# A fused attention and bilinear feed-forward kernel: spreading weight rounding, moving the denominators and an accumulating transfer, and computing T3 earlier

## The chip, the cores and the metric

The kernel runs on one core of a Trainium2 chip. The metric is device time in microseconds (us). The engines are named as in the profile: PE is TensorE (PEld its weight loads), DVE VectorE, ACT ScalarE, POOL GpSimd, SP SyncE, which here issues most DMA transfers. Every engine works through its own instructions in the order of the program; semaphores hold an instruction until its inputs and its buffer are free.

## The reference

Routing attention, then a bilinear feed-forward layer. Cut to what is computed:

```python
# q, k, v: (4, 8, 768, 64); centroids: (8, 16, 64)
q_assign = argmax(q_n . c_n); k_assign = argmax(k_n . c_n)   # nearest of 16 centroids
mask = q_assign[..., None] == k_assign[..., None, :]
scores = where(mask, q @ k.T / 8, -1e9)
attn = softmax(scores); x = (attn @ v) as (3072, 512)
a = x @ w_a; b = x @ w_b            # (512, 1536) each
out = (a * b) @ w_out               # (1536, 512)
```

## The kernel before

Attention goes by 16 pairs of heads (four to a batch of 768 rows), each in two halves of 384 queries with six score tiles (`j` = 0 to 5). A group, one round of the main loop (`g`), handles two score tiles, so a pair takes six groups and a batch 24. The score tile comes out of PSUM through an exponential into one of four buffers `pt`; one group later the tiles are multiplied with `v`, and summed into `acc` for the softmax's denominators. From the second batch of attention on, the feed-forward products of the batch before are strewn between the attention work (`ffn` is their queue). They are done by a Strassen-Winograd scheme with seven products in place of eight; its combined operands are called S1 to S4 (weights) and T1 to T4 (rows of x).

Sums of the exponentials. For the later pairs (`p >= HP`, the second batch on), the first two tiles are added on DVE and the other four by accumulating transfers that POOL issues:

```python
def add_up(u):
    p, hf, j = where(u)
    if j == 0 or j == NJ - 1 and p < HP:
        return
    ...
    if j == 1:
        nc.vector.tensor_tensor(out=acc, in0=probs[u - 1], in1=probs[u], op=ALU.add)
    else:
        nc.gpsimd.dma_start(out=acc, in_=probs[u], accum_op=ALU.add)     # L598
```

The denominators are the sums across partitions, by products with ones (L629), copied back by ACT (L634). The tile comes from `apart()`, which, once products are due, is one of the two score tiles:

```python
def denominators(p, hf):
    ps = apart()
    acc = accs.pop((p, hf))
    ...
            nc.tensor.matmul(out=ps[a * D:(a + 1) * D, 0:HB], lhsT=ones, rhs=t[:, a, :], ...)
    nc.scalar.activation(out=den, in_=ps[:, 0:HB], func=AF.Copy, accum_out=...)
```

Rounding of the weights: 36 parts of 128x512, which arrive as 64-bit values in one of two buffers `raw`. Four DVE operations and a POOL addition make the 32-bit value; `rest` has one buffer. ACT then inspects the sizes with two activations (`see_w`), which lets the load of the part after the next start:

```python
def round_w(i):
    ...
    nc.vector.tensor_scalar(out=wi, in0=hi, ...)                  # L280
    nc.vector.scalar_tensor_tensor(out=wi, in0=hi, in1=wi, ...)   # L283
    rest = wtp.tile([P, WN], FP32, name="rest")
    nc.vector.tensor_scalar(out=rest, in0=wi, ...)                # L287
    nc.vector.scalar_tensor_tensor(out=rest, in0=lo, in1=rest, ...)   # L290
    nc.gpsimd.tensor_tensor(out=w, in0=w, in1=rest, op=ALU.add)   # L292
    unseen.append(...)

def see_w():
    while unseen:
        ...
        nc.scalar.activation(out=size, in_=upper, func=AF.Abs)    # L304
        nc.scalar.activation(out=size, in_=size, func=AF.Relu, ...)   # L306
        load_w(i + 2)
```

Two of the seven products, with the takes (ACT copies a bank out, L830), the additions (DVE, L834) and the multiplications (POOL, L840). A bank is written again by the product two places later, once the copy has read it:

```python
def take(name, k, f):
    box[name] = place(k, f)
    nc.scalar.copy(out=box[name], in_=box["X"][:, 0:HB])
    see_w()
def add(name, bank):
    nc.vector.tensor_tensor(out=box[name], in0=box[name], in1=box[bank][:, 0:HB], op=ALU.add)
def done(name, k, f):
    if not is_a:
        nc.gpsimd.tensor_tensor(out=to, in0=to, in1=box[name], op=ALU.mult)
...
def p6():
    product("X", "S2", "T2", start=False)
    take("12", 1, i)
def p7():
    product("X", "S3", "T3", start=False)
    take("22", 1, i + N2); add("22", "Z"); done("22", 1, i + N2)
...
# order [p1, p2, p6, p5, p7, p3, p4]; in the first batch:
ps[1] = both(ps[1], lambda: combine_x(b, "T3"))    # T3 behind p2
ps[3] = both(lambda: combine_x(b, "T4"), ps[3])
```

The main loop, cut:

```python
due = {3 * i + 1: [i] for i in range(8)}
for i in range(8, len(w_parts)):
    due.setdefault(26 + int((i - 8) / 1.5), []).append(i)
...
for g in range(NG + 3):
    ...
    score(now)                       # products and exponentials
    check_inverses()
    for u in before: add_up(u)
    weigh(before)
    if g % 3 == late and 0 < g - late:
        denominators(*divmod(g // 3 - 1, 2))
    ready[l]()
    parts = due.get(g, [])
    def round_next():
        if parts or not ffn:
            see_w()
        if parts:
            round_w(parts.pop(0))
    round_next()
    if halved: todo.extend(normalize(*ph))      # DVE, DVE, DVE, then POOL multiplies xT (L661)
    if ffn:
        credit += ...
        while len(ffn) > least and credit > 0:
            cost, piece = ffn.popleft(); credit -= cost
            piece()
            if todo: todo.popleft()()
            round_next()
    else:
        credit = 0
    round_next()
    while todo: todo.popleft()()
    ...
```

Of the kernel before, what the change touches and what calls it, by code (L numbers as in the profile page):

```python
# [34 lines left out]
P = 128  # L35
# [107 lines left out]
def short_path(nc, tc, ctx, c, cn, centroids_in, casts, n_far, q, k, v,  # L143
# [121 lines left out]
    def load_w(i):  # L265
        if i >= len(w_parts):
            return
        raw = rawp.tile([P, WN], INT64, name="raw")
        nc.sync.dma_start(out=raw, in_=w_parts[i][1])
        raws[i] = raw  # L270

    def round_w(i):
        w = w_parts[i][0]
        wi = w.bitcast(INT32)
        raw = raws.pop(i)
        halves = lambda dt: raw.bitcast(dt).rearrange("p (n two) -> p n two", two=2)
        lo, hi = halves(UINT32)[:, :, 0], halves(INT32)[:, :, 1]


        nc.vector.tensor_scalar(out=wi, in0=hi, scalar1=3, scalar2=0x3FFFFFF8,  # L280
                                op0=ALU.logical_shift_left,
                                op1=ALU.bitwise_and)
        nc.vector.scalar_tensor_tensor(out=wi, in0=hi, scalar=SIGN_TOP, in1=wi,  # L283
                                       op0=ALU.bitwise_and, op1=ALU.bitwise_or)

        rest = wtp.tile([P, WN], FP32, name="rest")
        nc.vector.tensor_scalar(out=rest.bitcast(INT32), in0=wi,  # L287
                                scalar1=SIGN_EXP, scalar2=None,
                                op0=ALU.bitwise_and)
        nc.vector.scalar_tensor_tensor(out=rest, in0=lo, scalar=2.0 ** -52,  # L290
                                       in1=rest, op0=ALU.mult, op1=ALU.mult)
        nc.gpsimd.tensor_tensor(out=w, in0=w, in1=rest, op=ALU.add)  # L292
        unseen.append((i, halves(FP32)[:, :, 1]))

    unseen = []

    def see_w():

        while unseen:
            i, upper = unseen.pop()
            size = spare()[0].bitcast(BF16)[:, 3 * WN:4 * WN]
            nc.scalar.activation(out=size, in_=upper, func=AF.Abs)  # L304
            n = 4 * NPAIR + i
            nc.scalar.activation(out=size, in_=size, func=AF.Relu, scale=-STEEP,  # L306
                                 bias=edge[:, 0:1], accum_out=stat[:, n:n + 1])
            load_w(i + 2)

    NSTAT = 4 * NPAIR + len(w_parts)  # L310
    edge = zero.tile([P, 1], FP32, name="edge")
# [231 lines left out]

    probs, accs, O_of, den_of, xTs = {}, {}, {}, {}, {}
    unchecked = []
    todo = deque()
    UPP = 2 * NJ
    NU = NPAIR * UPP
# [34 lines left out]
# [5 lines that stand above are left out]
            accs[p, hf] = accp.tile([P, 2, HB], FP32, name="acc")  # L588
        acc = accs[p, hf]
        if p < HP:  # L590
            nc.vector.tensor_tensor(out=acc, in0=probs[u - 1] if j == 1 else acc,  # L591
                                    in1=probs[u], op=ALU.add)
            return
        if j == 1:
            nc.vector.tensor_tensor(out=acc, in0=probs[u - 1], in1=probs[u],  # L595
                                    op=ALU.add)
        else:
            nc.gpsimd.dma_start(out=acc, in_=probs[u], accum_op=ALU.add)  # L598

    def weigh(us):  # L600
        for u in us:
# [141 lines left out]
    def spare():  # L743
        if "spare" not in W:
            W["spare"] = [combp.tile([P, n], FP32, name=name) for name, n in (
                ("pair", 2 * WN), ("comb", 2 * P))]
        return W["spare"]
# [25 lines left out]
    def combine_x(b, name):  # L773
        x = xTs[b]
        l, r = {"T3": (x[:, 2:4, HB:S], x[:, 0:2, HB:S]),
                "T1": (x[:, 0:2, HB:S], x[:, 0:2, 0:HB]),
                "T2": (x[:, 2:4, HB:S], W["T1"]),
                "T4": (x[:, 2:4, 0:HB], W["T2"])}[name]
        nc.vector.tensor_tensor(out=W[name], in0=l, in1=r, op=ALU.subtract)

    def ffn_ups(b, h):
# [109 lines left out]
        for n, (combinations, ps) in enumerate(parts):  # L891
            if n == 0 and b:
                ps[0] = both(*combinations, ps[0])
                ps[2] = both(lambda: combine_x(b, "T4"), ps[2])
            elif n == 0:
                ps[1] = both(ps[1], lambda: combine_x(b, "T3"))
                ps[3] = both(lambda: combine_x(b, "T4"), ps[3])
            if n + 1 < len(parts):
                for i, step in enumerate(parts[n + 1][0], 4):
                    ps[i] = both(ps[i], step)  # L900
            pieces += [(2 * HB, f) for f in ps]
# [10 lines left out]
    def ffn_downs(b, h):  # L912
# [96 lines left out]

        def before():  # L1010
            see_w()
            assert not raws
            down_room()
            tiles[0][0]()
            combine_w("T1", "12", "11")
            combine_w("T2", "22", "T1")
# [13 lines left out]
    def both(*fs):  # L1030
        return lambda: [f() for f in fs]
# [5 lines left out]
    def early_steps():  # L1037
        combinations = []

        def begin():  # L1040
            early_room(h_first)
            steps, pieces = ffn_ups(0, h_first)
            ups_first.extend(pieces)
            combinations.extend(steps)

        last = HP * GPP
        return {last - 8: lambda: (begin(), combine_x(0, "T1")),
                last: lambda: [f() for f in combinations[0:2]],
                last + 1: lambda: combinations[2]()}

    def ffn_ready(p, hf):

        b, hp = divmod(p, HP)
        if hp < HP - 1 or hf == 0:
            return
        if b > 0:
            h = []

            ffn.insert(len(ffn) - FREE_ROOM, (0, lambda: (
                up_room(b), combine_x(b, "T3"), combine_x(b, "T1"))))  # L1060
            ffn.insert(len(ffn) - 1, (0, lambda: combine_x(b, "T2")))
            ffn.extend(ffn_ups(b, h)[1])
        else:
            h = h_first
            combine_x(0, "T2")
            ffn.extend(ups_first + plain_ups(0, h, range(NF - 4, NF)))
        ffn.extend(ffn_downs(b, lambda: h))

# [14 lines left out]

    due = {3 * i + 1: [i] for i in range(8)}
    for i in range(8, len(w_parts)):
        due.setdefault(26 + int((i - 8) / 1.5), []).append(i)
    early = early_steps()

    for _ in range(12):
        nc.tensor.matmul(out=idle[0:D, 0:D], lhsT=ones, rhs=ones, start=True,  # L1090
# [31 lines left out]
    for g in range(NG + 3):  # L1122
        p, l = divmod(g, GPP)
        if l == 0:
            ready = prep_steps(p + 1)
        now = (2 * g, 2 * g + 1)
        before = (2 * g - 2, 2 * g - 1)
        if g == 1:
            weigh(before)
        if 0 < g < NG:  # L1130
            score(now)
        check_inverses()
        if 0 < g <= NG:
            for u in before:
                add_up(u)
        if 1 < g <= NG:
            weigh(before)
        late = int(g > EARLY)
        if g % 3 == late and 0 < g - late:
            denominators(*divmod(g // 3 - 1, 2))  # L1140
        if g < NG:
            ready[l]()
        parts = due.get(g, [])
        if g in early:
            todo.append(early[g])

        def round_next():
            if parts or not ffn:
                see_w()
            if parts:  # L1150
                i = parts.pop(0)
                round_w(i)

        round_next()
        if g <= EARLY:
            first, second = 4, 1
        else:
            first, second = 5, 3 if g < NG else 2
        ph = {first: (p, 0), second: (p - 1, 1)}.get(l)
        halved = ph in den_of  # L1160
        if halved:
            todo.extend(normalize(*ph))
        if ffn:
            credit += PER_GROUP[(g > 2 * BG + 3) + (g > 3 * BG + 3)]
            least = FREE_ROOM if halved and ph[1] and (ph[0] + 1) % HP == 0 else 0
            while len(ffn) > least and credit > 0:
                cost, piece = ffn.popleft()
                credit -= cost
                piece()
                if todo:  # L1170
                    todo.popleft()()
                round_next()
        else:
            credit = 0
        round_next()
        while todo:
            todo.popleft()()
        if halved:
            ffn_ready(*ph)
        if l == 0 and p + 1 < NPAIR:  # L1180
            if p and not by_blocks(p + 1):
                prep_transpose(p + 1, 2)
            load(p + 2)
        if l == 4 and p + 1 < NPAIR and not by_blocks(p + 1):
            prep_onehot(p + 1, 0)
# [265 lines left out]
```

## Time and profile before

| | |
|---|---|
| time, median of 3 | 1055.83 us (1055.52 to 1056.8) |
| span of the profiled execution | 1052.8 us |
| PE busy | 1023.8 us, 97% |
| DVE, ACT, POOL busy | 55%, 32%, 24% |
| accumulating transfers `acc<-pt` | 96, 384 KB each, 4.0 us to landing in the median |
| mean granted clock of TensorE | 0.995 |

PE's busy share is so high that the reading goes by its idle time: which waits it has, where in the span, and which engine's queue ended them. A line of a timeline has the start in us, the duration, the engine, the line of the kernel, the operation, what it writes and reads, and in brackets how long its engine stood idle before it and what ended that. A line of the waits has who waited for whom, the total in us, how often, and the longest.

### The profile page before, as it was taken

Reading aid. Unit: us, or ns where it says so; the run is one execution under the profiler, and the core shown is the slowest. Engines: PE = TensorE matmul, PEld = TensorE weight load, DVE = VectorE, ACT = ScalarE, POOL = GpSimd, SP = SyncE. Lnnn points to the kernel's source line nnn. Section 1 sums busy time; section 2 is a strip of 40 time slices with the busy share of each in tenths; the row PEclk is TensorE's granted clock in tenths of the full one; section 3 lists DMA queues with packets and bytes.
Section 4 is the critical chain, followed back from the end, with each engine's and each line's share of the span. In section 5 each row is a group of like instructions: output and inputs, shape, how many; then the busy total and the mean of one; then the engine's idle time right before and its main releaser. Section 6 shows DMA issues by size and latency. Waiting matters only on the chain.

```text
span 1052.8 us, 17688 instructions
## 1 busy us (share of the span) xinstructions
PE 1023.8 (97%) x7094; PEld 499.5 (47%) x7094; DVE 579.2 (55%) x1098; ACT 336.5 (32%) x674; POOL 254.1 (24%) x251
## 2 busy tenths in 40 slices
PE   8999989989999999999999999999999999999997
PEld 5443333334445554444444655444444566444564
DVE  6668777786658345443545535444443635444552
ACT  5666544444542213333233121233232201111100
POOL 1112234354332112222324211232222110212100
PEclk9999989999999999999999999999999999999999
DMA  7334546857574463626243372533322320000000
GB/s 181 87 83 88 102 90 147 167 129 154 140 156 86 94 112 65 109 46 106 54 81 65 78 134 54 91 61 66 60 45 50 76 56 21 1 1 1 6 31 29
DMA packets 134346, 84.24 MB, mean 80 GB/s; under 512 B 108144, under 2 KB 117360, under 8 KB 134256
## 3 DMA queue, kind: packets, MB, share of 16 engines
q0 software_dynamic: 13824, 37.75, 19.8%
q1 hardware_dynamic: 120016, 44.85, 19.0%
q8 instruction: 58, 0.95, 0.4%
q10 hardware_dynamic: 416, 0.43, 0.1%
q14 instruction: 32, 0.26, 0.1%
HBM read 37.78 MB, written 6.29 MB: 42 GB/s over the span
## 4 chain that ended last, share of the span: by engine, by line
PE 80%; DMA 6%; DVE 6%; issue 4%; POOL 2%; ACT 2%; DVEq 0%; POOLq 0%; SPq 0%; ACTq 0%
PE m L692 54%; PE s L563 12%; PE O L606 10%; DMA acc<-pt 5%; PE s L629 1%; PE m L629 1%; PE s L378 1%; DVE acc L591 1%; ACT pt L572 1%; PE m L378 1%; POOL xT L661 0%; DVE acc L595 0%; POOL acc L598 0%; POOL h L840 0%; PE m L362 0%
## 5 line engine op out<-in xcount | busy, mean ns | idle before, releaser
L572 ACT ACTIVATE pt<-s 128x768 f32<-128x768 f32 x192 | 146.2, 808 | 191.1 <-PE s L563 142.6
L598 POOL DMA_DIRECT2D acc<-pt x96 | 82.8, 862 | 261.1 <-DMA acc<-pt 161.5
L606 PE MATMUL O<-pt,v 128*64 128x384 f32 x768 | 145.0, 499 | 0.0
L563 PE MATMUL s<-qkT 64*128 64x384 f32 x768 | 140.3, 484 | 0.0
L840 POOL TENSOR_TENSOR h<-h,ha 128x384 f32<-128x384 f32 x66 | 72.8, 1110 | 214.6 <-DVE ha L834 213.7
L834 DVE TENSOR_TENSOR ha<-ha,m 128x384 f32<-128x384 f32 x88 | 48.1, 549 | 126.7 <-PE m L692 100.9
L830 ACT COPY h<-m 128x384 f32<-128x384 f32 x88 | 42.2, 480 | 213.3 <-PE m L692 209.9
L834 DVE TENSOR_TENSOR h<-h,m 128x384 f32<-128x384 f32 x88 | 48.2, 547 | 100.9 <-PE m L692 73.5
L606 PEld LDWEIGHTS O<-pt,v 128*64 128x64 f32 x768 | 46.6, 136 | 85.8 <-issue 77.9
L692 PE MATMUL m<-wo_sb,h 128*64 128x256 f32 x768 | 86.7, 379 | 0.0
L692 PE MATMUL m<-xT,wa_sb 128*64 128x384 f32 x480 | 83.7, 487 | 2.7 <-DVE ha L834 2.5
L563 PEld LDWEIGHTS s<-qkT 64*128 64x128 f32 x768 | 71.0, 188 | 31.8 <-issue 0.9
L692 PE MATMUL m<-xT,wb_sb 128*64 128x384 f32 x480 | 83.1, 486 | 0.4 <-DVE h L834 0.4
L692 PE MATMUL m<-raw 128*64 128x384 f32 x432 | 78.9, 486 | 0.0
L692 PEld LDWEIGHTS m<-wo_sb,h 128*64 128x64 f32 x768 | 56.1, 137 | 29.1 <-issue 3.7
L661 POOL TENSOR_TENSOR xT<-xT,acc 128x384 f32<-128x384 f32 x32 | 35.2, 1099 | 133.4 <-DVE acc L656 84.1
L692 PE MATMUL m<-xT,h 128*64 128x256 f32 x576 | 64.6, 379 | 0.0
L692 PE MATMUL m<-xT,pair 128*64 128x384 f32 x352 | 64.5, 487 | 0.0
L830 ACT COPY ha<-m 128x384 f32<-128x384 f32 x66 | 31.6, 478 | 98.8 <-PE m L692 93.2
L692 PEld LDWEIGHTS m<-xT,wa_sb 128*64 128x64 f32 x480 | 34.9, 137 | 46.1 <-issue 33.2
L692 PEld LDWEIGHTS m<-xT,wb_sb 128*64 128x64 f32 x480 | 34.6, 137 | 43.5 <-issue 37.0
L692 PEld LDWEIGHTS m<-xT,h 128*64 128x64 f32 x576 | 42.1, 137 | 21.4 <-issue 1.6
(180 smaller groups left out, 1323.6 us busy)
## 6 DMA issues: line engine op xcount, KB each, us to landing
acc<-pt POOLq DMA_DIRECT2D x96, 384.0 KB, 4.0
raw<-in_moe_w_a_dram SPq DMA_DIRECT2D x12, 512.0 KB, 4.2
raw<-in_moe_w_b_dram SPq DMA_DIRECT2D x12, 512.0 KB, 3.7
raw<-in_moe_w_out_dram SPq DMA_DIRECT2D x12, 512.0 KB, 3.9
qk<-in_q_dram SPq DMA_DIRECT2D x48, 96.0 KB, 3.3
qk<-in_k_dram SPq DMA_DIRECT2D x48, 96.0 KB, 3.7
v<-in_v_dram SPq DMA_DIRECT2D x24, 192.0 KB, 3.9
out_dram<-rest SPq DMA_DIRECT2D x24, 128.0 KB, 1.7
```

The costliest lines, as they stand in the source:

```text
L378: nc.tensor.matmul(out=ps[32 * kq:32 * kq + 32, 0:HB], lhsT=cTb[:, hp, :], rhs=qkTs[p][:, kq * HB:(kq + 1) * HB], start=True, stop=True)
L563: nc.tensor.matmul(out=s[:, a, 0:HB], lhsT=Ts[p][r, S + j * P:S + (j + 1) * P], rhs=Ts[p][r, hf * HB:(hf + 1) * HB], start=start, stop=not ...
L572: nc.scalar.activation(out=pt, in_=s[:, :, 0:HB], func=AF.Exp, scale=SCALE)
L591: nc.vector.tensor_tensor(out=acc, in0=probs[u - 1] if j == 1 else acc, in1=probs[u], op=ALU.add)
L598: nc.gpsimd.dma_start(out=acc, in_=probs[u], accum_op=ALU.add)
L606: nc.tensor.matmul(out=O_of[0][a * D:(a + 1) * D, 0:HB], lhsT=vs[p][:, a, j, :], rhs=probs[u][:, a, :], start=(j == 0), stop=(j == NJ - 1))
L629: nc.tensor.matmul(out=ps[a * D:(a + 1) * D, 0:HB], lhsT=ones, rhs=t[:, a, :], start=(n == 0), stop=(n == len(terms) - 1))
L661: nc.gpsimd.tensor_tensor(out=x, in0=x, in1=den, op=ALU.mult)
L692: nc.tensor.matmul(out=ps[half], lhsT=lhsT[:, half], rhs=rhs, **kw)
L830: nc.scalar.copy(out=box[name], in_=box["X"][:, 0:HB])
L834: nc.vector.tensor_tensor(out=box[name], in0=box[name], in1=box[bank][:, 0:HB], op=ALU.add)
L840: nc.gpsimd.tensor_tensor(out=to, in0=to, in1=box[name], op=ALU.mult)
```

## The change

Five parts, all of them moves in the order of the same instructions:

- The rounding of a weight part is split in two steps of two DVE operations each; one step (two behind a long product) goes behind each product. The inspection on ACT is split in two as well; while no products are due, one of its steps goes to each group. The parts are due slightly sooner (1.6 to a group in place of 1.5).
- The denominators are put behind the group's second product, where there are products.
- Of each two accumulating transfers of a group the second is issued at the group's end, so that POOL does not stand before it while multiplications wait.
- T3 of the first batch is computed straight behind T2, before its first product.
- The lists that hold this are renamed (`rounding`, `at_the_end`).

```diff
     def round_w(i):
+
         w = w_parts[i][0]
         wi = w.bitcast(INT32)
-        raw = raws.pop(i)
...
+        def first():
+            see_w()
+            hi = halves(INT32)[:, :, 1]
+            nc.vector.tensor_scalar(out=wi, in0=hi, scalar1=3, scalar2=0x3FFFFFF8, ...)
+            nc.vector.scalar_tensor_tensor(out=wi, in0=hi, scalar=SIGN_TOP, in1=wi, ...)
+
+        def second():
+            rest = wtp.tile([P, WN], FP32, name="rest")
+            nc.vector.tensor_scalar(out=rest.bitcast(INT32), in0=wi, ...)
+            nc.vector.scalar_tensor_tensor(out=rest, ..., in1=rest, ...)
+            nc.gpsimd.tensor_tensor(out=w, in0=w, in1=rest, op=ALU.add)
+            unseen.extend(see_steps(i))
+
+        return [first, second]
...
+    def see_steps(i):
+        size = spare()[0].bitcast(BF16)[:, 3 * WN:4 * WN]
+        def first():
+            ...
+            nc.scalar.activation(out=size, in_=upper[:, :, 1], func=AF.Abs)
+        def second():
             n = 4 * NPAIR + i
             nc.scalar.activation(out=size, in_=size, func=AF.Relu, ...)
+            del raws[i]
             load_w(i + 2)
+        return [first, second]
+
+    def see_w(steps=None):
+        for _ in range(len(unseen) if steps is None else min(steps, len(unseen))):
+            unseen.popleft()()
...
         else:
-            nc.gpsimd.dma_start(out=acc, in_=probs[u], accum_op=ALU.add)
+            add = lambda: nc.gpsimd.dma_start(out=acc, in_=probs[u],
+                                              accum_op=ALU.add)
+            add() if j % 2 == 0 else at_the_end.append(add)
...
             elif n == 0:
-                ps[1] = both(ps[1], lambda: combine_x(b, "T3"))
                 ps[3] = both(lambda: combine_x(b, "T4"), ps[3])
...
             combine_x(0, "T2")
+            combine_x(0, "T3")
             ffn.extend(ups_first + plain_ups(0, h, range(NF - 4, NF)))
...
-        due.setdefault(26 + int((i - 8) / 1.5), []).append(i)
+        due.setdefault(26 + int((i - 8) / 1.6), []).append(i)
...
-        if g % 3 == late and 0 < g - late:
-            denominators(*divmod(g // 3 - 1, 2))
+        halves = [divmod(g // 3 - 1, 2)] if g % 3 == late and 0 < g - late else []
+        def sums_across():
+            while halves:
+                denominators(*halves.pop())
+        if not ffn:
+            sums_across()
+        pieces = 0
...
-        parts = due.get(g, [])
+        for i in due.get(g, []):
+            rounding.extend(round_w(i))
...
         def round_next():
-            if parts or not ffn:
-                see_w()
-            if parts:
-                i = parts.pop(0)
-                round_w(i)
-        round_next()
+            if rounding:
+                rounding.popleft()()
+        if not ffn:
+            see_w(1)
+            round_next()
...
                 piece()
                 if todo:
                     todo.popleft()()
-                round_next()
+                for _ in range(cost // HB // 2):
+                    round_next()
+                pieces += 1
+                if pieces == 2:
+                    sums_across()
         else:
             credit = 0
-        round_next()
+            round_next()
+        sums_across()
         while todo:
             todo.popleft()()
+        while at_the_end:
+            at_the_end.pop(0)()
```

More of the change, by code (lines that the diff above doesn't have):

```diff
@@ L274, in round_w @@
         wi = w.bitcast(INT32)
-        raw = raws.pop(i)
[L276 to L304, printed above, removed]
+        halves = lambda dt: raws[i].bitcast(dt).rearrange(
+            "p (n two) -> p n two", two=2)
+        def first():
+            see_w()
+            hi = halves(INT32)[:, :, 1]
+            nc.vector.tensor_scalar(out=wi, in0=hi, scalar1=3, scalar2=0x3FFFFFF8,
+                                    op0=ALU.logical_shift_left,
+                                    op1=ALU.bitwise_and)
+            nc.vector.scalar_tensor_tensor(
+                out=wi, in0=hi, scalar=SIGN_TOP, in1=wi, op0=ALU.bitwise_and,
+                op1=ALU.bitwise_or)
@@ new lines, in second @@
+        def second():
+            rest = wtp.tile([P, WN], FP32, name="rest")
+            nc.vector.tensor_scalar(out=rest.bitcast(INT32), in0=wi,
+                                    scalar1=SIGN_EXP, scalar2=None,
+                                    op0=ALU.bitwise_and)
+            nc.vector.scalar_tensor_tensor(
+                out=rest, in0=halves(UINT32)[:, :, 0], scalar=2.0 ** -52, in1=rest,
+                op0=ALU.mult, op1=ALU.mult)
+            nc.gpsimd.tensor_tensor(out=w, in0=w, in1=rest, op=ALU.add)
+            unseen.extend(see_steps(i))
@@ L305, in see_w @@
+        return [first, second]
+    unseen = deque()
+    def see_steps(i):
+        size = spare()[0].bitcast(BF16)[:, 3 * WN:4 * WN]
+        def first():
+            upper = raws[i].bitcast(FP32).rearrange("p (n two) -> p n two", two=2)
+            nc.scalar.activation(out=size, in_=upper[:, :, 1], func=AF.Abs)
+        def second():
             n = 4 * NPAIR + i
@@ L545, in short_path @@
     unchecked = []
+    at_the_end = []
     todo = deque()
@@ L1011, in before @@
             see_w()
-            assert not raws
+            assert not raws and not rounding
             down_room()
@@ L1085, in short_path @@
     for i in range(8, len(w_parts)):
-        due.setdefault(26 + int((i - 8) / 1.5), []).append(i)
+        due.setdefault(26 + int((i - 8) / 1.6), []).append(i)
     early = early_steps()
+    rounding = deque()
     for _ in range(12):
```

## The prediction

> **What bounds the kernel now.** I read the busy shares first, then the waits of TensorE alone, then the busy time by stages, and last the timeline around the longest waits.
>
> ```profile
> PE 1023.8 (97%) x7094; PEld 499.5 (47%) x7094; DVE 579.2 (55%) x1098; ACT 336.5 (32%) x674; POOL 254.1 (24%) x251
> ...
> PE m L692 <- DVE h L779: 5.6, 1, 5.6
> PE s L629 <- DMA acc<-pt: 4.9, 4, 1.8
> PE m L692 <- DVE ha L834: 2.5, 2, 2.3
> PE s L563 <- ACT pt L572: 2.0, 6, 0.4
> ```
>
> TensorE (PE) has 1052.8 - 1023.8 = 29 us of idle time in the whole span. 7.4 of them lie at its end and 2.5 before the first real product, so a reordering can win some 19 us at most, plus what a slow clock costs. It can lose more. The stages (start:end, span, then busy PE, PEld, DVE, ACT, POOL, clock, DMA share, GB/s) say where the idle time lies:
>
> ```profile
> 118.00:142.00 24.00, 18.38 (x106) 7.65 (x104) 16.84 (x31) 9.20 (x17) 7.08 (x7) 0.86 0.79 151
> 142.00:300.00 158.00, 150.78 (x938) 64.66 (x936) 114.04 (x194) 75.50 (x156) 65.99 (x61) 1.00 0.62 137
> ...
> 414.00:820.00 406.00, 406.00 (x2726) 188.31 (x2724) 188.79 (x374) 118.12 (x234) 106.81 (x109) 1.00 0.41 73
> ```
>
> 5.6 us are idle at 118 to 142, 7.2 at 142 to 300 while weights are rounded, none at all at 414 to 820. The last row matters: there the change has nothing to win, only to lose. The timeline shows the longest wait:
>
> ```profile
> 130.72 1.58 POOL L292 TENSOR_TENSOR wa_sb<-wa_sb,rest 128x512 f32<-128x512 f32 x1
> 132.34 0.43 DVE L287 TENSOR_SCALAR rest<-wb_sb 128x512 int32<-128x512 int32 x1 [1.93 <-POOL wa_sb L292]
> 132.80 0.69 DVE L290 SCALAR_TENSOR_TENSOR rest<-raw,rest 128x512 f32<-128x512 uint32 x1
> 133.41 0.55 DVE L834 TENSOR_TENSOR h<-h,m 128x384 f32<-128x384 f32 x1
> ...
> 133.57 1.26 POOL L292 TENSOR_TENSOR wb_sb<-wb_sb,rest 128x512 f32<-128x512 f32 x1 [1.27 <-DVE rest L290]
> 133.87 1.77 DVE L779 TENSOR_TENSOR h<-xT 128x768 f32<-128x768 f32 x1
> ...
> 135.79 2.83 PE L692 MATMUL m<-h,pair 128*64 128x384 f32 x8 [5.62 <-DVE h L779]
> ```
>
> VectorE (DVE) holds the second half of a rounding because its one buffer `rest` is still read by GpSimd (POOL), POOL had stood behind an accumulating transfer, and T3 stands in DVE's queue behind both.
>
> **What the Trainium skill says.** "TensorE: Matmul & The Clock Gate", Part 1, has the clock halved after an idle window of about 3.4 us. The trace agrees: behind the 5.62 us wait the same eight matmuls take 2.83 us instead of 1.46, and the stage's mean clock is 0.86. "DMA: Bandwidth & Descriptors", Anatomy of one DMA, puts semaphore waits on the issuing sequencer; agreed, POOL sat idle 161.5 us for its own transfers before the next ones. The same section's fixed 2.0 us plus bytes by 436e9 would make an estimated 2.9 us of 393 KB; the trace has 3.9 at least and 4.0 in the median, and I use 4.0. "GPSIMD Engine Reference", Specifications, says its SBUF interfaces are shared with VectorE; the T3 subtraction above took 1.77 us beside a POOL addition, its twin T2 0.96 with POOL issuing.
>
> **The change part by part.** A group is one round of the main loop: scores 1.72 us, weighing 1.44 us, sometimes denominators 0.65 us, then about five products of 1.29 us (all from the chain). No matmul is added or removed, so the sum is one of waits.
>
> *T3 behind T2, and rounding in two steps, 118 to 142.* T2 ends at 126.6. T3 straight behind it, at up to 1.77 us, is there at 128.4; the product that uses it can start at 130.0, after its predecessors. The 5.6 us wait goes, and with it the half clock: 2.83 - 1.46 = 1.4, and 2.63 - 1.72 = 0.9 for the next scores. 7.9 in all; DVE was busy 16.84 us here and its work has to fit a shorter stage, so I count -7.
>
> *The split inspection, before 118.* ScalarE's two activations per part (0.67 and 0.91 with the readout) come one per group while no products are due. They stand before the exponentials that delay TensorE at 36, 63 and 89; each time it loses 0.37 + 0.53 us from start to start against its usual pace. 3 x 0.9 = 2.7, I count -2.5.
>
> *Rounding split, 142 to 300.* Four DVE operations in a row are 0.42 + 0.69 + 0.43 + 0.69 = 2.2 us before an addition that TensorE needs. At 158, 189, 191 and 224 TensorE comes 0.3 + 0.4 + 0.3 + 2.5 = 3.5 us late for this reason. Half a rounding is 1.1 us, so -2.5.
>
> *Denominators behind two products.* TensorE gets 2.6 us more before it needs the sums. Where the last transfer keeps its place this removes the wait: 1.3 at 278, 0.5 at 367, 1.5 at 855.6, together -3.3.
>
> *The second transfer at the group's end.* Here is the cost. Its issue now stands on POOL behind every multiplication of its group. In the steady stage POOL reaches those late:
>
> ```profile
> 445.53 0.87 POOL L598 DMA_DIRECT2D acc<-pt  x1 [3.60 <-DMA acc<-pt]
> ...
> 454.84 2.31 POOL L840 TENSOR_TENSOR h<-h,ha 128x384 f32<-128x384 f32 x2 [2.27 <-DVE ha L834]
> 457.12 0.99 POOL L661 TENSOR_TENSOR xT<-xT,acc 128x384 f32<-128x384 f32 x1
> ```
>
> The transfer of 445.53 moves to 458.1 and lands at 462.1. The next group starts at 454.75, so its denominators, after 1.72 + 1.44 + 2.6 us, are due at 460.5: a new wait of 1.6 us. A second path is the buffer `pt`: there are four, and the group's second exponential reuses the one that the transfer reads. In the group at 474.6 the multiplication before the transfer ends at 476.4, landing 480.4; the exponential moves from 476.6 to 480.4, and with its 0.81 us and two copies of 0.48 the bank is free at 482.2 instead of 479.7, while a product wants it at 480.3: a wait of 1.9 us. I went so through all group ends of 414 to 820: behind the 28 delayed transfers eleven groups show a wait, at 415, 424, 455, 475, 516, 662, 672, 702, 723, 763 and 785, of 0.7, 0.9, 1.6, 1.9, 0.7, 0.7, 0.8, 1.6, 0.3, 0.7 and 1.2 us, together 11.1, always by these two rules. Since a wait in one place also gives the late engine time, I count +10. In 142 to 300 the same happens behind the rounding's additions; the exponentials at 174 and 205 already wait for a transfer (2.8 and 2.1 us) and will wait longer. I put +5.5 for about four groups, the least sure term.
>
> Sum: -7 - 2.5 - 2.5 - 3.3 + 10 + 5.5 = +0.2, that is 1055.8 + 0.2 = 1056.0 us.
>
> **The rivals.** *The gains stand alone.* If POOL, no longer blocked amid a group, reaches its multiplications earlier than in this trace, the late transfers are issued earlier too and the two plus terms shrink to a few us: -15 + 4 gives 1045. For it speaks that POOL is busy 24% only and waited 161.5 us for transfers; against it, that in 414 to 820 the multiplications waited for DVE, which waits for products, not for POOL. *The transfers cost more.* Where the weights still stream, landing took up to 8.3 us instead of 4.0. Then six or seven groups of 142 to 300 lose 2 to 3 us each, and the sum is near +15, 1070. For it speaks the list of ScalarE's waits, 13.4 us for these transfers already. *DVE becomes the bound* at 118 to 200: busy 70% at 118 to 142 and 72% at 142 to 300, it would be at 16.84 of some 16 us in the first stage alone; that would eat half of the -7, 1060.
>
> **Range and chances.** The gains are bounded by 19 us of idle time and are read off directly; the losses are inferred from positions in a queue and could be a third or twice of it. Taking -15 + 4 and +15 less a little as the ends gives 1044 to 1068. To be 2% faster it would need 1034.7, more than all idle time that can be won: 2%. To be 2% slower it would need 1077, the losses tripled: 3%. The rest, 95%, is within 2%; the sign is open.
>
> **What would show it.** T3: no PE wait for the subtraction, clock 1.00 in the stage behind 118. Inspection: the waits for `pt` before 118 gone. The transfer: the stage behind 414 no longer fully busy, new waits of PE for `acc` transfers and for copies of ScalarE, and ScalarE's wait of exponentials for transfers far above 13.4 us, with POOL's wait for its own transfers below 161.5. If that stage stays fully busy, the step from POOL's order to late landings is wrong, and the time is near 1045.

## The result, and the profile after

The changed kernel takes 1107.59 us (median; 1104.62 to 1110.36) where the kernel before takes 1055.67 beside it: a ratio of 1.0498, with a 95% interval of 1.0456 to 1.054. It is slower by 52 us. The prediction was 1056.0 within 1044 to 1068.

The page of the kernel after, first the busy times and then the clock row of its slices:

```profile
PE 1038.2 (94%) x7094; PEld 503.3 (46%) x7094; DVE 577.7 (52%) x1098; ACT 334.0 (30%) x674; POOL 253.3 (23%) x251
...
PEclk9999989898998999999999999999999999999999
```

The matmuls are the same 7094, but TensorE is busy 14.4 us longer, and idle 1102.9 - 1038.2 = 64.7 us instead of 29.0. These 14.4 + 35.7 make up the 50.1 us between the two profiled spans. Its waits (total, number, longest, in us):

```profile
PE s L652 <- DMA acc<-pt: 24.2, 14, 5.8
PE m L715 <- ACT ha L853: 22.3, 9, 7.9
```

The 5.6 us for the T3 subtraction, first in this list before, are gone. In their place stand two new heads: denominators (L652) that wait for an accumulating transfer, 24.2 us instead of 4.9, and products (L715) that wait for a copy out of PSUM on ScalarE, 22.3 us instead of 1.1. All engines' waits show the other side of it, first after:

```profile
ACT pt L593 <- DMA acc<-pt: 111.7, 28, 8.2
POOL acc L619 <- DMA acc<-pt: 107.8, 28, 6.2
```

and the same waits before, with that of the products:

```profile
POOL acc L598 <- DMA acc<-pt: 161.5, 42, 8.0
ACT pt L572 <- DMA acc<-pt: 13.4, 7, 3.0
PE m L692 <- ACT ha L830: 1.1, 1, 1.1
```

POOL does wait less for its own transfers (107.8 us instead of 161.5), which is what the change wanted, and ScalarE's exponentials wait 111.7 us for them instead of 13.4. The transfers themselves are no slower: in the median they land after 4.0 us in both kernels.

Windows by the clock no longer hold the same work, so I cut both traces at the same groups: at the starts of the 27th, 29th, 44th, 56th and 96th run of score matmuls, which are 117.8, 138.6, 295.3, 414.7 and 825.0 before, and 115.0, 128.5, 314.2, 445.4 and 875.2 after. Stretches 3 to 5 of after (columns as in the stages of before):

```profile
128.50:314.20 185.70, 157.49 (x924) 66.52 (x924) 120.33 (x204) 74.90 (x155) 68.07 (x63) 0.93 0.56 125
314.20:445.40 131.20, 123.14 (x916) 64.67 (x914) 66.17 (x127) 33.49 (x68) 24.82 (x27) 0.97 0.46 89
445.40:875.20 429.80, 414.59 (x2768) 192.31 (x2768) 190.33 (x377) 118.34 (x235) 106.29 (x109) 1.00 0.39 70
```

and the same work before:

```profile
138.60:295.30 156.70, 149.48 (x921) 64.19 (x920) 114.33 (x197) 72.81 (x149) 65.32 (x61) 0.99 0.61 136
295.30:414.70 119.40, 118.96 (x914) 63.18 (x912) 68.41 (x126) 34.83 (x71) 24.50 (x27) 1.00 0.52 102
414.70:825.00 410.30, 410.30 (x2766) 191.34 (x2764) 190.34 (x377) 118.75 (x235) 106.95 (x109) 1.00 0.41 74
```

Stretch 3, in which weights are rounded, is 29 us longer, and in it TensorE has 28.2 us of idle time instead of 7.2 and 8.0 us more busy time at a clock of 0.93. Stretch 5, the steady stage, fully busy before, has 15.2 us of idle time. I use these cuts for every kernel below. Differences from before, each from one profile:

| kernel (what of the change it has) | to 1 | 2 | 3 | 4 | 5 | rest |
|---|---|---|---|---|---|---|
| before, us | 117.8 | 20.7 | 156.8 | 119.4 | 410.3 | 227.8 |
| after | -2.9 | -7.2 | +28.9 | +11.8 | +19.4 | 0.0 |
| e1, all but the late transfer | -3.0 | -7.2 | +3.0 | +0.5 | +0.6 | -1.3 |
| e2, the late transfer alone | 0.0 | -1.0 | +20.9 | +28.3 | +72.3 | +14.1 |
| e3, after, late transfer from another tile | -2.6 | -7.2 | +30.7 | +4.6 | +12.7 | -0.4 |
| e4, after, denominators early | -2.9 | -7.2 | +41.9 | +35.1 | +70.4 | +14.1 |
| e5, T3 alone | -0.3 | -7.2 | +3.2 | +0.9 | 0.0 | -0.1 |
| e6, rounding alone | -2.7 | -7.2 | +21.1 | +4.5 | 0.0 | 0.0 |
| e7, denominators alone | -0.2 | 0.0 | -3.8 | +0.5 | +0.6 | -1.1 |
| e8, after, transfer behind second product | -2.7 | -7.2 | +8.7 | +9.3 | +0.6 | -1.3 |
| e10, e3 with denominators at the group's end | -2.7 | -7.2 | +7.5 | +11.3 | +8.2 | -0.3 |
| e11, no second transfer | -2.6 | -7.2 | -8.6 | +0.5 | +0.6 | -0.8 |
| e12, e1 with whole roundings | -2.8 | -7.2 | +1.0 | +1.9 | +0.6 | -1.2 |
| e14, after with whole roundings | -2.2 | -7.2 | +23.4 | +5.8 | +21.2 | 0.0 |

The longest wait shows how one late transfer grows. The timeline of after, from 207 us on:

```profile
207.26 0.69 DVE L297 SCALAR_TENSOR_TENSOR rest<-raw,rest 128x512 f32<-128x512 uint32 x1
...
208.03 1.38 POOL L300 TENSOR_TENSOR wb_sb<-wb_sb,rest 128x512 f32<-128x512 f32 x1 [4.22 <-DVE rest L297]
...
209.35 0.91 POOL L619 DMA_DIRECT2D acc<-pt  x1
...
213.43 0.81 ACT L593 ACTIVATE pt<-s 128x768 f32<-128x768 f32 x1 [7.63 <-DMA acc<-pt]
...
214.13 0.47 ACT L639 COPY xT<-O 128x384 f32<-128x384 f32 x1
214.49 0.50 ACT L853 COPY h<-m 128x384 f32<-128x384 f32 x1
...
214.86 0.68 ACT L315 ACTIVATE pair<-raw 128x512 bf16<-128x512 f32 x1
...
216.30 0.46 ACT L853 COPY ha<-m 128x384 f32<-128x384 f32 x1
...
216.81 2.83 PE L715 MATMUL m<-h,comb 128*64 128x384 f32 x8 [7.94 <-ACT ha L853]
```

Read it from the bottom. TensorE waited 7.94 us for a PSUM bank that ScalarE empties. ScalarE came late with that copy because two copies and an inspection (L315 and its second half) had piled up behind an exponential (L593), which waited 7.63 us for its buffer `pt`. A transfer was still reading that buffer, because POOL had issued it only at 209.35, behind the rounding's addition (L300), and that addition had itself waited 4.22 us for VectorE. Not all of the 7.94 us is the late transfer's, as e1 shows.

### The profile page after: what moved, and what is told of

It is laid out like the page before. It is cut to its first block, busy times and chain, and to the rows that moved or that the text cites. A ratio compares the mean times of both kernels' runs of the same rounds, so it can differ in the third digit from the quotient of the medians.

```text
span 1102.9 us, 17679 instructions
## 1 busy us (share of the span) xinstructions
PE 1038.2 (94%) x7094; PEld 503.3 (46%) x7094; DVE 577.7 (52%) x1098; ACT 334.0 (30%) x674; POOL 253.3 (23%) x251
## 5 line engine op out<-in xcount | busy, mean ns | idle before, releaser
L593 ACT ACTIVATE pt<-s 128x768 f32<-128x768 f32 x192 | 149.4, 809 | 294.0 <-PE s L584 121.8
L619 POOL DMA_DIRECT2D acc<-pt x96 | 82.8, 866 | 148.2 <-DMA acc<-pt 107.8
L715 PE MATMUL m<-wo_sb,h 128*64 128x256 f32 x768 | 86.9, 379 | 0.0
L715 PE MATMUL m<-xT,wa_sb 128*64 128x384 f32 x480 | 86.5, 500 | 0.0
L715 PE MATMUL m<-xT,wb_sb 128*64 128x384 f32 x480 | 83.3, 486 | 0.1
L715 PE MATMUL m<-raw 128*64 128x384 f32 x432 | 79.2, 487 | 3.0 <-ACT ha L853 1.6
L715 PEld LDWEIGHTS m<-wo_sb,h 128*64 128x64 f32 x768 | 56.1, 137 | 29.5 <-issue 4.0
L715 PE MATMUL m<-xT,h 128*64 128x256 f32 x576 | 64.6, 379 | 0.0
L715 PE MATMUL m<-xT,pair 128*64 128x384 f32 x352 | 64.4, 487 | 0.0
L715 PEld LDWEIGHTS m<-xT,wa_sb 128*64 128x64 f32 x480 | 37.1, 141 | 43.5 <-issue 31.4
L715 PEld LDWEIGHTS m<-xT,wb_sb 128*64 128x64 f32 x480 | 34.4, 137 | 43.5 <-issue 39.0
L715 PEld LDWEIGHTS m<-xT,h 128*64 128x64 f32 x576 | 42.1, 137 | 21.4 <-issue 1.8
```

The lines of the kernel that those rows point to most:

```text
L593: nc.scalar.activation(out=pt, in_=s[:, :, 0:HB], func=AF.Exp, scale=SCALE)
L619: add = lambda: nc.gpsimd.dma_start(out=acc, in_=probs[u], accum_op=ALU.add)
L715: nc.tensor.matmul(out=ps[half], lhsT=lhsT[:, half], rhs=rhs, **kw)
```

## The experiments

The theory: what costs the time is the second transfer, landing late because it stands behind all of its group's POOL work, and it acts through two readers, the buffer `pt` and the denominators. The rivals: the later denominators do the harm (B), or the split rounding does, by crowding DVE, POOL and ScalarE (A).

**e1: the second transfer at once, the rest as in after.**

```diff
-            add() if j % 2 == 0 else at_the_end.append(add)
+            add()
```

> The kernel after, with one part undone: both accumulating transfers of a group are issued where the first is, none at the group's end. Theory (the late second transfer holds the exponentials' buffer and the denominators): all of the loss and more goes, the other parts' gains stand alone, 1043 us (1038 to 1048); exponentials wait for transfers under 20 us in all, and TensorE's clock is back at 0.99 or above. Rival A (the split rounding puts POOL's additions and VectorE late, whatever the transfers do): most of the loss stays, above 1080 us. Rival B (the denominators behind two products hold a score tile): the loss stays in part, 1065 to 1090 us.

Measured: 1047.32 us, a ratio of 0.9948 [0.9928, 0.9968] (here and below: to the kernel before, run beside it, with the 95% interval). One line takes back the whole loss. Against e1, after is longer by 25.9 us in stretch 3, 11.3 in stretch 4, 18.8 in stretch 5 and 1.3 behind it: 57.3 us, the price of the late transfer among the other parts. The 39.1 us for which exponentials still wait for transfers are more than I expected, and the gain is 4 us short. TensorE still waits 7.7 us for ScalarE's copies, most of it in the group of the longest wait above:

```profile
198.87 0.81 ACT L593 ACTIVATE pt<-s 128x768 f32<-128x768 f32 x1 [4.31 <-DMA acc<-pt]
...
202.28 2.19 PE L715 MATMUL m<-h,comb 128*64 128x384 f32 x6 [4.63 <-ACT ha L853]
```

So the `pt` path is there without any transfer moved late, and of the 7.94 us in after the late transfer added 3.3.

**e2: before, with nothing but the late transfer.**

```diff
-            nc.gpsimd.dma_start(out=acc, in_=probs[u], accum_op=ALU.add)
+            add = lambda: nc.gpsimd.dma_start(out=acc, in_=probs[u],
+                                              accum_op=ALU.add)
+            add() if j % 2 == 0 else at_the_end.append(add)
...
+        while at_the_end:
+            at_the_end.pop(0)()
```

> The kernel before, with this part alone: the second accumulating transfer of a group is issued at the group's end. Theory: the loss appears by itself, and is larger than in the kernel after because the denominators stand ahead of the products: 1110 us (1095 to 1135), with TensorE's waits for acc transfers well above the 24 us of the kernel after. Rival A: it needs the split rounding to do harm; the time stays under 1075 us.

Measured: 1191.49 us, 1.1333 [1.1299, 1.1367]. The largest of TensorE's waits in e2:

```profile
PE s L632 <- DMA acc<-pt: 93.3, 23, 6.4
```

The direction was right, the size far too small: the denominators, which in this kernel stand ahead of the products, wait 4 us each.

**e3: after, the late transfer reads another tile.** It adds weights in place of the group's exponentials, so the denominators hold foreign numbers for two of six tiles; the transfers, their size and their order stay, but nobody who reuses `pt` waits for the late one.

```diff
-            add = lambda: nc.gpsimd.dma_start(out=acc, in_=probs[u],
+            src = probs[u] if j % 2 == 0 else wa_sb[:, 0, 0:2 * HB].rearrange(
+                "p (a t) -> p a t", a=2)
+            add = lambda: nc.gpsimd.dma_start(out=acc, in_=src,
                                               accum_op=ALU.add)
```

> The kernel after, with the late transfer reading a finished stretch of the weights in place of pt: same size, same order, same sum buffer, but it no longer holds the exponentials' buffer (the denominators then hold weights in place of two of six tiles). Theory: the buffer is the larger of two paths; ScalarE's waits for transfers fall from 112 us to under 15, TensorE's waits for ScalarE's copies (23.7 us) go, and with them most of the half clock: 1072 us (1062 to 1082); the waits of the denominators (24 us) stay. If the denominators are the larger path: above 1092 us.

Measured: 1092.49 us, 1.0385 [1.0365, 1.0405]. Its first wait of TensorE:

```profile
PE s L654 <- DMA acc<-wa_sb: 40.5, 18, 6.8
```

That is above my range, and just where I had put the denominators as the larger path. No wait for ScalarE's product copies is left, yet only 15 us come back: the denominators' waits grew from 24.2 to 40.5. The two paths lie side by side, and who takes one away uncovers the other. In stretch 3 nothing is won (+30.7); the `pt` path was worth 11.8 - 4.6 = 7.2 us in stretch 4 and 19.4 - 12.7 = 6.7 us in stretch 5.

**e4: after, with the denominators ahead of the products again.**

```diff
-        if not ffn:
-            sums_across()
+        sums_across()
```

> The kernel after, with the denominators back ahead of the products and all else kept. Theory: they are needed 2.6 us sooner, while the transfer is as late as before, so TensorE's wait for acc transfers grows from 24 us to about 60: 1135 us (1120 to 1150). Rival B (moving the denominators did the harm): it gets faster, below 1085 us.

Measured: 1207.99 us, 1.1489 [1.146, 1.1518], with 103.0 us of waits for the denominators. Both are far above what I expected, as in e2. Rival B falls: beside late transfers the later denominators save 100 us.

**e5: T3 behind T2 alone.**

```diff
-                ps[1] = both(ps[1], lambda: combine_x(b, "T3"))
...
             combine_x(0, "T2")
+            combine_x(0, "T3")
```

> The kernel before, with T3 behind T2 alone. In the kernel with the second transfer at once the stretch of the first products took 7.7 us less than before. If T3's place makes it alone: 1045 us (1043 to 1048), and the 5.6 us wait for the subtraction is gone. If the split rounding is needed with it, because VectorE's backlog then ends some later addition late: 1049 to 1053 us.

Measured: 1048.59 us, 0.9944 [0.9927, 0.9961], just outside both of the expected ranges. Stretch 2 is 7.2 us shorter, as predicted, but stretch 3 gives back 3.2: soon after its start products wait 1.3 us for another subtraction on VectorE (L779) and 1.6 us for an addition (L834, 0.4 us at its one wait before). The second half of the expectation, a backlog on VectorE, is thus partly seen.

**e6: the rounding and inspection in steps alone**, that is, after without its other three parts.

```diff
-            add() if j % 2 == 0 else at_the_end.append(add)
+            add()
...
+                ps[1] = both(ps[1], lambda: combine_x(b, "T3"))
...
-            combine_x(0, "T3")
...
-        if not ffn:
-            sums_across()
+        sums_across()
```

> The kernel before, with the split rounding and inspection alone (and 1.6 parts to a group). It brings 2.7 us before 118 us by the split inspection. The groups behind the first products took 4.3 us more in the kernel with the second transfer at once than in the kernel before. If the split rounding does that (POOL's additions come later and stand ahead of both transfers): about 1052 us, -2.7 and some +4 and a part of the T3 wait, with ScalarE's wait of exponentials for transfers near 39 us instead of 13. If it relieves VectorE as meant: 1045 us or less.

Measured: 1068.31 us, 1.0127 [1.0107, 1.0147]. It also removes the wait of stretch 2, but loses 21 us in stretch 3. Its waits there (window 128.8 to 306.7):

```profile
PE s L652 <- DMA acc<-pt: 11.8, 4, 4.0
PE m L715 <- ACT ha L853: 7.7, 3, 5.1
```

These are the same two paths, here without a late transfer. I put it down to the order of POOL: spread out, the roundings' additions come later there and stand ahead of the transfers. At 133.92, for instance, an addition (L300) has waited 3.95 us for VectorE, and a transfer follows it at 135.14; that this holds for the whole loss was not shown. So rival A is partly right, and only there. With the denominators moved and T3 behind T2 as well (e1) no more than +3.0 is left.

**e7: the denominators behind the second product alone.**

```diff
+        if not ffn:
+            sums_across()
+        pieces = 0
...
                 round_next()
+                pieces += 1
+                if pieces == 2:
+                    sums_across()
```

> The kernel before, with the denominators behind the second product alone. TensorE's wait for acc transfers (4.9 us) goes but for under 1 us, nothing else moves: 1048.5 us (1046 to 1051). If holding a score tile later does harm (rival B), the time is 1052 us or more and TensorE's score products wait for ScalarE's copy.

Measured: 1053.21 us over 20 runs, 0.9992 [0.9983, 1.0002]: no difference that can be measured. Its profile has none of before's waits for transfers, and a span 3.9 us shorter, mostly in stretch 3, but the execution profiled (1050.56) is among the fastest of its runs (1050.18 to 1056.72), and their median does not bear the gain out. The mark that I had named for rival B is there, though small: the time is above 1052 us, and score products wait 1.8 us, in four places, for ScalarE's copy of the denominators. One profile does not settle a term of 3 us in stretch 3, here or in the other rows of the table.

**e8: the second transfer behind the group's second product.**

```diff
                 if pieces == 2:
                     sums_across()
+                    while at_the_end:
+                        at_the_end.pop(0)()
```

> The kernel after, with the second transfer issued behind the group's second product instead of at its end; all else kept. Theory (the harm is lateness alone): fewer of POOL's additions and multiplications stand ahead of it, by about three products (3.9 us), so both readers wait less: 1062 us (1050 to 1075), ScalarE's wait of exponentials for transfers 40 to 80 us (112 in the kernel after, 39 with it at once).

Measured: 1061.97 us, 1.0059 [1.0039, 1.0079]. As expected, with 47.4 us of exponentials' waits: half-way late costs nothing in stretch 5 (+0.6), while stretches 3 and 4 are 18 us longer than before.

**e10: e3, with the denominators at the group's end**, so that both readers are out of the way; the denominators again hold foreign numbers.

```diff
-                if pieces == 2:
+                if pieces == 99:
                     sums_across()
```

> The kernel after, with the late transfer reading a finished stretch of the weights in place of pt, and with the denominators at the group's end instead of behind the second product. Both readers of the late transfer are then out of its way: neither the exponentials' buffer nor the denominators need it soon. Theory: the two paths are the whole loss, so the time is within 6 us of the 1047 us of the kernel with the second transfer at once: 1041 to 1053 us, TensorE's waits for acc transfers under 6 us (40 us with the other source alone). If the late order on POOL does harm in another way (multiplications behind waiting transfers): above 1060 us.

Measured: 1071.42 us, 1.0172 [1.0151, 1.0194]. That is in the range that I had named for another harm, multiplications behind waiting transfers, but no wait of TensorE in its trace is ended by a multiplication of POOL. Its waits of TensorE in stretch 5 (423.7 to 842.2) are a single line:

```profile
PE s L584 <- ACT acc L659: 5.6, 13, 0.5
```

No wait of the two paths is left there. This one is the experiment's own: the late denominators hold a PSUM bank that the next scores need. So in stretch 5 no loss by another path is seen. In stretch 3 weakening both brings back 21.4 of the 28.9 us, where taking one away brought back nothing; the two are not quite gone there (4.9 us of waits for copies and 4.4 us for transfers). What e10 loses in stretch 4 is mostly its own wait again (5.4 us) with a slow clock (0.97), so it says little of after there.

**e11: the second transfers left out**, so two of six tiles are missing from the denominators.

```diff
-            add() if j % 2 == 0 else at_the_end.append(add)
+            if j % 2 == 0:
+                add()
```

> The kernel after, with the second transfers left out (two of six tiles are missing from each denominator). Nothing then waits for a late transfer, and POOL issues half as many. Theory: all of the loss of the kernel after hangs on them: 1040 us (1036 to 1045), below the 1047 us with both at once. If POOL's split additions alone make the first transfers late as well: 1047 us or more.

Measured: 1036.2 us, 0.9813 [0.9784, 0.9841]. Without them the rest of the change is a gain everywhere up to stretch 3. The second transfers cost e1 11 us even when they are issued at once, nearly all in stretch 3, where e1 has 9.3 us of idle time and e11 0.7: the exponentials' waits for transfers fall from 39.1 us to 1.5, and TensorE's waits for ScalarE's product copies are gone.

**e12 and e14: whole roundings**, in e12 with the second transfer at once, in e14 with it late.

```diff
-        return [first, second]
+        return [lambda: (first(), second())]
```

> The kernel after, with the second transfer at once and each weight part rounded in one piece again, behind one product; the split inspection, the later denominators and T3 stay. If the split rounding is what cost 4 us in the groups behind the first products: 1043 us (1040 to 1046), less than the 1047 us with the rounding split. If it did not, 1047 us or more.

> The kernel after with the rounding in one piece again, the second transfer still at the group's end. Theory: in the groups with rounding the late transfer stands behind POOL's additions, which stand behind VectorE's second half steps; with whole roundings these come one product earlier, and the loss of 41 us over the kernel with the transfer at once shrinks there, while the 20 us behind 414 us stay: 1085 us (1070 to 1098). If the rounding's form does not matter for it: 1100 us or more.

Measured: e12 1047.51 us, 0.9922 [0.9893, 0.9951], the same as e1: its waits for ScalarE's copies shrink from 7.7 to 1.5 us, and waits for VectorE (4.1 + 1.7 + 1.3) take their place. e14 1094.34 us, 1.0359 [1.0327, 1.0392], within its range: the split adds 13 us to the loss when the transfers are late, and 38 us are there without it. The fastest complete versions are e12, e5 and e1, under 1% below before; their intervals overlap.

## Why the prediction was wrong, point by point

**The mechanism was right.** POOL's order, the late landing, the two paths, and the signs named for them (the stage behind 414 no longer fully busy, both new waits, 13.4 us rising, 161.5 falling) are all in the trace. Two groups were worked out in detail. The one at 702.3 before starts at 747.4 after, and the timeline of after reads:

```profile
747.51 2.31 POOL L863 TENSOR_TENSOR h<-h,ha 128x384 f32<-128x384 f32 x2 [2.26 <-DVE ha L857]
...
749.78 1.00 POOL L684 TENSOR_TENSOR xT<-xT,acc 128x384 f32<-128x384 f32 x1
...
750.73 0.87 POOL L619 DMA_DIRECT2D acc<-pt  x1
...
754.81 0.87 PE L652 MATMUL s<-acc,ones 128*64 128x384 f32 x4 [1.58 <-DMA acc<-pt]
```

1.58 us, predicted 1.6. The one at 474.6 before starts at 509.7 after, with its `pt` path:

```profile
510.54 1.00 POOL L863 TENSOR_TENSOR h<-h,ha 128x384 f32<-128x384 f32 x1 [0.88 <-DVE ha L857]
...
511.48 0.87 POOL L619 DMA_DIRECT2D acc<-pt  x1
...
515.48 0.81 ACT L593 ACTIVATE pt<-s 128x768 f32<-128x768 f32 x1 [3.71 <-DMA acc<-pt]
...
516.55 0.50 ACT L853 COPY ha<-m 128x384 f32<-128x384 f32 x1
...
517.10 1.51 PE L715 MATMUL m<-raw 128*64 128x384 f32 x8 [1.57 <-ACT ha L853]
```

1.57 us, predicted 1.9.

**The sum.** Between the two profiles lie +50.1 us. The parts other than the late transfer make -7.2 of them (e1 against before; -5.1 in the medians), where the prediction had -15.3; the late transfer makes +57.3 (after against e1), where it had +15.5.

**The failed step: "+5.5 for about four groups", the price of late transfers in 142 to 300.** Measured there (after against e1): +25.9. Six groups waited, not four, but the size of a wait was further off. TensorE's waits of after in stretch 3:

```profile
PE m L715 <- ACT ha L853: 19.3, 4, 7.9
PE s L652 <- DMA acc<-pt: 8.8, 2, 5.8
```

Six waits, 28.1 us, 4.7 each, where I had put 1.4 each. The idle time of this stretch is 9.3 us in e1 and 28.2 in after, so 18.9 us are new. I had named the two existing waits of exponentials and let them "wait longer", but did not follow one such group to its end, as I had done for the steady stage. In all six groups a rounding's addition (L300) stands on POOL ahead of the late transfer, and it had itself waited 1.9 to 4.7 us for VectorE (4.22 us in the fence above); behind the exponential ScalarE has, in part of them, inspections to do besides the copies. The landing itself took 3.9 to 4.5 us in five of the six, and 7.3 in the sixth.

And the sum had **no term for the slow clock**: the clock that "TensorE: Matmul & The Clock Gate", Part 1, has halved after an idle window of about 3.4 us was counted for the gain, but it holds for new waits too. Behind the 7.94 us wait eight matmuls take 2.83 us instead of 1.46. The other 7.0 of the 25.9 us are longer busy time of TensorE (157.5 us against 150.5 in e1), at a clock of 0.93 against 0.98.

**No term at all for 300 to 414.** There the late transfer cost 11.3 us (after against e1). The prediction has only a wait of denominators at 367 there, as a gain.

**"+10" behind 414: measured +18.8.** Each of the eleven groups named shows a wait; they sum to 11.6 us, predicted 11.1. Six further groups wait 3.6 us, and TensorE's busy time is 4.3 us longer, though the clock stays at 1.00; the last section says where that comes from. The discount from 11.1 to 10, because "a wait in one place also gives the late engine time", was wrong: the trace shows the waits at the same size to the end of the stretch (1.24 us at 690, 0.76 at 842).

**T3 and rounding, -7: measured -7.2** in stretch 2, in every kernel that has either T3 behind T2 or the split rounding. Each of the two alone is enough (e5, e6).

**Inspection, -2.5: measured -2.9** ahead of stretch 2, with the waits for `pt` there gone.

**Rounding split, -2.5: not found.** The waits of products for VectorE in stretch 3 are down from 2.9 us to 0.5 in e1, as meant, but waits for ScalarE's copies take their place, and with whole roundings (e12) the time is the same. Alone it does harm: +21.1 in stretch 3 in e6. I infer that the same POOL additions, spread out, hold up the transfers. How much of e6's loss is POOL's order and how much VectorE's was not separated.

**Denominators, -3.3: not found in the timed runs** (e7), though its profile has -3.9. Four new waits for ScalarE's copy (1.8 us) take back part of the 4.9 us that go. Their value lies elsewhere: 100 us once the transfers are late.

**The rivals.** "The transfers cost more" was the true one, with its six or seven groups of 142 to 300, but at 4.7 us each and not 2 to 3; its reason, a landing of up to 8.3 us, fits one group of the six. "DVE becomes the bound" fell: in stretch 2 of after TensorE is busy for all of its 13.5 us. "To be 2% slower it would need the losses tripled" was reckoned wrongly: with the gains of -15.3 kept, 1077 us takes 36.5 us of losses, 2.4 times the 15.5 predicted, close to the double that the range allowed. The 3% given to it was a statement on my own estimate and not on the kernel: the least sure term was nearly five times as large.

## What to carry to other kernels

Before a transfer is moved later on an in-order queue, list everyone who waits for it, those who read its target and those who reuse its source, and look at what stands ahead of it on that queue at its worst place, not at its usual one. A stage in which TensorE has no idle time and the full clock can only lose by such a move, and a wait long enough to slow the clock costs more than itself (18.9 us of new idle time came with 7.0 us of longer busy time in stretch 3). A measure against a wait is worth what the wait is worth at that time: the later denominators brought nothing measurable alone and 100 us beside the late transfers, and with two paths to the same wait, removing one may bring nothing.

## What the runs showed of the hardware that was not expected

The idle time that a profile shows understates short waits. In stretch 5 of after, at a granted clock of 1.00, 19 waits with 15.2 us of idle time made the work 19.4 us longer. It does not follow that the matmuls ran slower. In a flow of products the records of TensorE overlap: four denominators' matmuls at 457.81 in the kernel before last 0.81 us, but the next product starts 0.64 us after them. Ahead of a wait this overlap, 0.17 us in the median, is lost and its time counts as busy. For 19 waits I estimate 3.2 us of the missing 4.2 from it; part of the rest lies in slightly longer records behind waits (0.87 us instead of 0.81). As the profiler models the ends of matmuls, this is a matter of how waits are counted, from start to start.

In this kernel accumulating transfers into one buffer wait for each other, so a transfer can be late though it is issued in its first place. In e1 POOL stood 4.91 us for the transfer before, until 194.20, and the exponential at 198.87 waited 4.31 us for the transfer issued then. Leaving 48 of 96 out (e11 against e1) shortened stretch 3 by 12 us.
